# First attention of a linear-attention and two-MLP kernel: another order of its query steps and first transfers

## The chip, the cores and the metric

The kernel runs on one NeuronCore of one Trainium2 chip. The metric is the device time of one execution in microseconds (us); the times shown are medians of several runs. Engines are named as in the profile: PE (TensorE, matrix products), DVE (VectorE), ACT (ScalarE), POOL (GpSimd) and SP (SyncE, which here issues all transfers).

## The reference, cut to what matters

Linear attention with a feature map, and then two MLPs. Inputs are float32 for q, k, v and `w_phi`; the weights of the MLPs come as float64.

```python
# q, k, v: (4, 8, 576, 64); w_phi: (64, 128)
def phi(x):
    proj = einsum('bhsd,df->bhsf', x, w_phi)
    proj = proj - max(abs(proj), axis=-1, keepdims=True)
    return concatenate([exp(proj), exp(-proj)], axis=-1)
q_p, k_p = phi(q), phi(k)
kv  = einsum('bhsf,bhsd->bhfd', k_p, v);  z = sum(k_p, axis=2)
num = einsum('bhsf,bhfd->bhsd', q_p, kv)
den = einsum('bhsf,bhf->bhs', q_p, z)[..., None] + 1e-06
x = (num / den) as (2304, 512)
x = leaky_relu(x @ w_in, 0.01) @ w_out          # 512 -> 2048 -> 512
out = (silu(x @ w_gate) * (x @ w_val)) @ w3     # 512 -> 1536 -> 512
```

## The kernel before, in words

The work is cut by batch: four batches `b` of 576 tokens, each with eight heads in `NP = 4` pairs `j` (pair 0 to 3; two heads of 64 fill the 128 partitions). A batch's attention runs first over the keys (`k_steps`) and then over the queries (`q_steps`). The attention of batch 0 stands alone at the start of the program, at line 959 (`steps = k_steps(0) + q_steps(0)`); the attention of each later batch is spread over the MLP units of the batch before it, where PE always has other work.

**Keys of batch 0.** For each pair and each of five token tiles `s`: a projection of k with `w_phi` on PE (L161, into a bank of the PSUM pool `psm`, tag `pm`, 4 banks), the greatest absolute value (L166) and a subtraction (L59) on DVE, two exponentials on ACT (L177, L178), and two products with v that gather k'v and z in one bank of the pool `psa`, tag `pa`, 4 banks (L202). A pair ends with a copy (`kvz`, ACT), four transposes on PE (L240, `k_tr`) and a copy (`kvh`, ACT).

**Queries of batch 0.** For each pair: five projections on PE (`q_front`, L301, `pm` banks), each with a maximum on DVE (L304, into `mq`); then `q_m` turns the maxima into a row (`mrow`, L316 to L321, DVE, one buffer). Then, for two halves `t` of 288 tokens and the two heads `h`: `q_exp` multiplies the weights with the queries a second time, now with tokens along the free axis (L372, `pa` bank), takes the row off (L373) and makes two exponentials on ACT (L375, L376); `q_num` makes numerator and denominator (L393, `pa` bank), and ACT writes the denominator (L396). `q_fin` ends a half on DVE: transpose, reciprocal, transpose (L401, L403, L405), two products that free the two `pa` banks (L411), and the split of x in a high and a low part (`cp` on ACT into `xh`, `sub` on DVE into `xl`, L59). `xh` and `xl` of a pair are one fourth of the inner dimension of the first MLP layer.

**Weights.** Every weight block of 128 x 512 comes as float64 and is made float32 by ACT (L511, L512) and DVE (L513, L514, L519), then stored (`kept`, L524) and split (L541 on ACT, L59 on DVE). While the first attention runs, eight blocks of the gate weights (`early`, tag `gp`) and the first blocks of `w_in` (tag `wi`, loaded at L497) go this way. The MLP's products are made at L579, in `pm` banks, always in parts high x high, high x low, low x high.

**What sets the order.** The code gives an order of emission; the framework's scheduler, with priorities from that order and a timeline of its own, then fixes the order in which each engine has its instructions. An engine runs its instructions in that order. `early` stands under a lower priority than its place. In `q_steps` the order of emission is, for each pair: five projections, the maxima, the load of the next pair's queries, then the four exponential steps with the numerators one step behind. The queries and keys of a pair land in `raw`, a tag with two buffers; so the load of a pair can start when the pair two before it has made its last product from it. All loads and stores go through SP's queue in one order. At the start, SP issues k of pair 0 (L115), `w_phi` (L117) and three pieces of v (L123).

## Time and profile before

| | us |
|---|---|
| median of 3 timed runs | 1099.75 (1099.22 to 1103.96) |
| profiled execution | 1096.49 |
| its span, first to last instruction | 1094.7 |
| first matmul | 4.03 |
| PE busy, of the span | 1065.8 |
| DVE busy | 822.9 |
| ACT busy | 640.4 |
| granted TensorE clock | 1.0 in all 40 slices |

A share of the whole span is an average over stages of different kinds. The first attention fills about the first 88 us; the MLPs, with the other three attentions among them, fill the rest. In the first part PE, DVE and ACT all have work, and which of them is late changes from stage to stage; this is read from the busy times by stretch and from the waits in the timeline. A PE that is busy is not a PE at its peak, as matmuls are pipelined and their ends are modelled.

### The profile page before, as it was taken

How to read it: one execution, taken by the hardware profiler on the slowest of the kernel's cores; microseconds unless marked ns; L12 is line 12 of the kernel's file. 1: busy time of each engine (PE TensorE's matmuls, PEld its weight loads, DVE VectorE, ACT ScalarE, POOL GpSimd, SP SyncE). 2: the span in 40 equal slices, each digit the busy share in tenths (PEclk: the TensorE clock that was granted, in tenths of full speed). 3: DMA queues.
4: the chain of work that ended last, by engine and by line, in shares of the span. 5: the costliest groups of instructions: out<-in, count | busy, mean ns of one | idle time of the engine just before them, and what ended most of it. 6: DMA issues, size and time to landing. Idle time of an engine off the chain costs nothing.

```text
span 1094.7 us, 20495 instructions
## 1 busy us (share of the span) xinstructions
PE 1065.8 (97%) x7608; PEld 1027.0 (94%) x7608; DVE 822.9 (75%) x1801; ACT 640.4 (58%) x1455; POOL 6.8 (1%) x28
## 2 busy tenths in 40 slices
PE   8889999899999999999999999999999999999998
PEld 6668999889989999999999999999999999999998
DVE  7997787889999877678687877757778653558473
ACT  7768976757756786647545366434554345426441
POOL 1000000000000000000000000000000000000000
PEclk9999999999999999999999999999999999999999
DMA  9736766345654865567483888787652657548642
GB/s 331 240 94 188 217 194 219 127 144 169 194 183 146 333 249 190 186 265 271 150 313 118 304 309 285 274 280 257 230 174 78 225 202 282 201 148 288 238 140 78
DMA packets 96402, 233.02 MB, mean 213 GB/s; under 512 B 20144, under 2 KB 20400, under 8 KB 96304
## 3 DMA queue, kind: packets, MB, share of 16 engines
q1 hardware_dynamic: 96304, 231.72, 61.6%
q8 instruction: 60, 0.98, 0.4%
q14 instruction: 38, 0.31, 0.1%
HBM read 163.00 MB, written 68.68 MB: 212 GB/s over the span
## 4 chain that ended last, share of the span: by engine, by line
PE 79%; DVE 7%; DMA 7%; ACT 3%; issue 2%; SPq 1%; DVEq 0%; ACTq 0%
PE pm L579 57%; PE pa L707 9%; DMA wr<-kept 4%; PE pa L393 4%; PE pa L202 3%; DMA wi<-in_w_dram 2%; PE pa L161 2%; PE pm L707 1%; DVE wr L514 1%; DVE wr L519 1%; DMA wi<-in_wv_dram 1%; PE pm L301 1%; DMA vhl<-parts 1%; PE pa L346 1%; DVE wr L59 1%
## 5 line engine op out<-in xcount | busy, mean ns | idle before, releaser
L579 PE MATMUL pm<-xh,wi 128*128 128x288 f32 x1920 | 408.1, 298 | 3.0 <-DVE es L618 2.2
L579 PE MATMUL pm<-gp,wo 128*128 128x288 f32 x2352 | 349.0, 297 | 7.3 <-DVE acc L644 7.1
L579 PEld LDWEIGHTS pm<-gp,wo 128*128 128x128 f32 x2352 | 323.4, 188 | 11.7 <-DVE acc L644 8.4
L579 PEld LDWEIGHTS pm<-xh,wi 128*128 128x128 f32 x1920 | 313.8, 188 | 7.9 <-DVE es L618 2.8
L579 PE MATMUL pm<-xl,wi 128*128 128x288 f32 x960 | 284.1, 297 | 0.0
L579 PEld LDWEIGHTS pm<-xl,wi 128*128 128x128 f32 x960 | 180.4, 188 | 2.0 <-issue 0.8
L644 DVE TENSOR_TENSOR acc<-pm,acc 128x288 f32<-128x288 f32 x160 | 70.1, 451 | 43.8 <-PE pm L579 43.1
L59 DVE TENSOR_TENSOR gp<-es,gp 128x576 fp32r<-128x576 f32 x98 | 73.6, 751 | 13.5 <-ACT gp L62 12.6
L62 ACT ACTIVATE gp<-es 128x576 fp32r<-128x576 f32 x98 | 68.0, 696 | 26.8 <-DVE es L625 23.9
L541 ACT ACTIVATE wi<-wr 128x512 fp32r<-128x512 f32 x80 | 51.1, 645 | 23.0 <-DMA wr<-kept 8.8
L59 DVE TENSOR_TENSOR wi<-wr,wi 128x512 fp32r<-128x512 f32 x80 | 54.6, 684 | 11.2 <-ACT wi L541 10.6
L59 DVE TENSOR_TENSOR fl<-ff,fh 128x512 fp32r<-128x512 f32 (+1 forms) x72 | 50.7, 714 | 13.2 <-ACT fh L62 12.2
L512 ACT ACTIVATE wi<-wi 128x512 int32<-128x512 uint32 x60 | 42.3, 704 | 28.1 <-DMA wi<-in_w_dram 14.3
L396 ACT ACTIVATE dn<-pa 64x288 f32<-64x288 f32 x64 | 26.1, 407 | 46.2 <-PE pa L393 45.4
L511 ACT ACTIVATE wr<-wi 128x512 f32<-128x512 f32 x60 | 41.7, 699 | 15.7 <-DMA wi<-in_w_dram 7.3
L605 ACT ACTIVATE es<-pm 128x288 f32<-128x288 f32 x96 | 39.7, 424 | 13.2 <-PE pm L579 12.6
L62 ACT ACTIVATE fh<-ff 128x512 fp32r<-128x512 f32 (+1 forms) x72 | 46.9, 670 | 0.6
L519 DVE TENSOR_TENSOR wr<-wr,wi 128x512 uint16<-128x512 uint16 x60 | 44.8, 748 | 0.4
L202 PE MATMUL pa<-ff,pk 128*128 128x256 f32 (+1 forms) x160 | 42.8, 383 | 1.5 <-issue 1.1
L513 DVE TENSOR_SCALAR wr<-wr 128x512 int32<-128x512 int32 x68 | 28.4, 419 | 18.7 <-ACT wr L511 18.6
L62 ACT ACTIVATE acc<-pm 128x288 f32<-128x288 f32 x64 | 26.4, 441 | 26.4 <-PE pm L579 26.1
L59 DVE TENSOR_TENSOR wo<-wr,wo 128x512 fp32r<-128x512 f32 x56 | 37.4, 681 | 5.5 <-ACT wo L541 3.9
(171 smaller groups left out, 1954.8 us busy)
## 6 DMA issues: line engine op xcount, KB each, us to landing
wi<-parts SPq DMA_DIRECT2D x80, 512.0 KB, 4.7
wr<-kept SPq DMA_DIRECT2D x116, 256.0 KB, 4.8
wo<-parts SPq DMA_DIRECT2D x49, 512.0 KB, 5.5
wi<-in_w_dram SPq DMA_DIRECT2D x44, 512.0 KB, 4.3
parts<-wi SPq DMA_DIRECT2D x40, 512.0 KB, 5.8
kept<-wr SPq DMA_DIRECT2D x68, 256.0 KB, 4.0
parts<-wo SPq DMA_DIRECT2D x28, 512.0 KB, 6.2
sums<-wr SPq DMA_DIRECT2D x40, 256.0 KB, 3.6
```

The costliest lines, as they stand in the source:

```text
L59: dve.tensor_tensor(out=o, in0=a, in1=b, op=ALU.subtract)
L62: act.activation(o, a, AF.Copy)
L202: pe.matmul(ps[:, 256 * h : 256 * h + 256], v[:n, h].rearrange("p a d -> p (a d)"), part[b, j, s][:n, h].rearrange("p a f -> p (a f)"), st ...
L393: pe.matmul(ps, w, x, start=(i == 0), stop=(i == len(ops) - 1))
L511: act.activation(t, high.bitcast(F32), AF.Abs, scale=REBIAS)
L512: act.activation(low, low.bitcast(U32), AF.Copy, scale=2.0**-29)
L519: dve.tensor_tensor(out=t16, in0=t16, in1=e16, op=ALU.add)
L541: i = act.activation(t[:, 0], r, AF.Copy)
L579: m = pe.matmul(ps, w, x[:, c], start=(i == 0), stop=(i == n - 1))
L605: act.activation(o, i, AF.Prelu, alpha=0.01)
L644: dve.tensor_tensor(out=acc[o][:, t], in0=ps, in1=acc[o][:, t], op=ALU.add)
L707: m = pe.matmul(ps, a, b, start=start and n == 0, stop=stop and n == 5, skip_group_check=True)
```

## The change

`load_k` issues `w_phi` ahead of the first keys, and these in two parts of 256 and 320 columns. `q_m` writes the row of pairs 1 and 3 into a buffer of the tag `es` (5 buffers) and that of pairs 0 and 2 into the one `mrow` buffer. `q_steps` (for batch 0 alone, the others use `q_steps_t`) emits the projections and maxima of pair j + 1 between the exponential steps of pair j, and loads the queries of pair j + 2 in the last of these steps; the first three steps of the queries are emitted with the last three steps of the keys. The diff, cut to its core:

```diff
     def load_k(b, j):
         raw["k", b, j] = t = T([P, S], F32, "raw", 2)
-        nc.sync.dma_start(out=t, in_=kT[b, j])
-        if not (b or j):
+        if b or j:
+            nc.sync.dma_start(out=t, in_=kT[b, j])
+        else:
             nc.sync.dma_start(out=wbd.rearrange("p h f -> p (h f)"), in_=w_phi)
+            nc.sync.dma_start(out=t[:, 0 : OFF[2]], in_=kT[b, j, :, 0 : OFF[2]])
+            nc.sync.dma_start(out=t[:, OFF[2] :], in_=kT[b, j, :, OFF[2] :])
...
-        r = mrow[b, j] = T([P, 18, 32], F32R, "mrow", 1)
+        r = mrow[b, j] = T([P, 18, 32], F32R, *(("es", 5) if j % 2 else ("mrow", 1)))
...
+        seq = [fronts(0, 0, 1), load(1) + fronts(0, 2, 3), fronts(0, 4) + maxima(0)]
+        last = []
         for j in range(NP):
-            seq.append([lambda j=j: q_front(b, j, 0), lambda j=j: q_front(b, j, 1)])
-            seq.append([lambda j=j: q_front(b, j, 2), lambda j=j: q_front(b, j, 3)])
-            nxt = (lambda j=j: load_q(b, j + 1)) if j + 1 < NP else (lambda: load_k(b + 1, 0) if b + 1 < B else None)
-            seq.append([lambda j=j: q_front(b, j, 4), lambda j=j: q_m(b, j), nxt])
...
+            seq.append(last + exps(j, 0, 0) + fronts(j + 1, 0, 1))
+            seq.append(exps(j, 1, 0) + nums(j, 0, 0) + fronts(j + 1, 2, 3))
+            seq.append(exps(j, 0, 1) + nums(j, 1, 0) + fronts(j + 1, 4))
+            seq.append(exps(j, 1, 1) + nums(j, 0, 1) + maxima(j + 1) + load(j + 2))
+            last = nums(j, 1, 1)
+        return seq + [last]
...
-    steps = k_steps(0) + q_steps(0)
+
+    one, two = k_steps(0), q_steps(0)
+    steps = one[:-3] + [a + b for a, b in zip(one[-3:], two[:3])] + two[3:]
```

Of the instructions, one transfer is added, and none is taken away; what the scheduler makes of the new emission is seen in the engines' orders. Line numbers after the change are higher by 3 from `load_k` on and by 12 from `q_steps_t` on (L304 is the projection L301, L375 and L376 are L372 and L373, L396 is L393, L243 is L240, L378 and L379 are the exponentials, L399 is L396, L523 and L524 are L511 and L512, L414 is L411). A name with its number is a buffer; `raw_403` and `raw_404` hold the queries of pair 0, `raw_477` and `raw_456` those of pair 1.

PE at the seam from keys to queries, before:

```order
L202 MATMUL pa_400<-ff_438,pk_340 128x256 x2
L240 MATMUL pa_448<-cst_sb,kvz_446 128x128 x4
L372 MATMUL pa_479<-raw_403,wbd 128x288
L372 MATMUL pa_485<-raw_403,wbd 128x288
L301 MATMUL pm_555<-wbd,raw_477 128x256
L301 MATMUL pm_559<-wbd,raw_477 128x256
L301 MATMUL pm_562<-wbd,raw_477 128x256
L301 MATMUL pm_565<-wbd,raw_477 128x256
L373 MATMUL pa_479<-mrow_475,sel 128x288
L373 MATMUL pa_485<-mrow_475,sel 128x288
```

and after:

```order
L205 MATMUL pa_401<-ff_439,pk_341 128x256 x2
L304 MATMUL pm_486<-wbd,raw_456 128x256
L304 MATMUL pm_490<-wbd,raw_456 128x256
L304 MATMUL pm_504<-wbd,raw_456 128x256
L304 MATMUL pm_507<-wbd,raw_456 128x256
L243 MATMUL pa_464<-cst_sb,kvz_454 128x128 x4
L375 MATMUL pa_480<-raw_404,wbd 128x288
L376 MATMUL pa_480<-mrow_478,sel 128x288
L375 MATMUL pa_493<-raw_404,wbd 128x288
L376 MATMUL pa_493<-mrow_478,sel 128x288
```

Four projections of pair 1 moved from behind the first score products of pair 0 to ahead of the last key pair's transposes.

DVE at the end of pair 1's first half (`pm_785` to `pm_795` before, `pm_686` to `pm_717` after, are projections of pair 3; `wr_847` and `wr_882` are weights in conversion), before:

```order
L321 TENSOR_TENSOR mrow_695<-mt_693,cst_sb 128x576
L405 STREAM_TRANSPOSE rb_630<-rc_628 128x288
L514 SCALAR_TENSOR_TENSOR wr_847<-gp_845,wr_847 128x512
L411 TENSOR_TENSOR xf_632<-pa_601,rb_630 64x288
L411 TENSOR_TENSOR xf_632<-pa_622,rb_630 64x288
L304 TENSOR_REDUCE mq_787<-pm_785 128x2
```

and after:

```order
L324 TENSOR_TENSOR mrow_651<-mt_649,cst_sb 128x576
L406 RECIPROCAL rc_612<-t_175_610 128x9
L531 TENSOR_TENSOR wr_882<-wr_882,gp_880 128x512
L307 TENSOR_REDUCE mq_688<-pm_686 128x2
L408 STREAM_TRANSPOSE rb_614<-rc_612 128x288
L404 STREAM_TRANSPOSE t_196_669<-dn_645 128x288
L307 TENSOR_REDUCE mq_688<-pm_690 128x2
L525 TENSOR_SCALAR wr_937<-wr_937 128x512
L307 TENSOR_REDUCE mq_688<-pm_714 128x2
L307 TENSOR_REDUCE mq_688<-pm_717 128x2
L414 TENSOR_TENSOR xf_616<-pa_589,rb_614 64x288
L414 TENSOR_TENSOR xf_616<-pa_606,rb_614 64x288
```

The two products that finish the half moved behind four maxima of pair 3.

ACT at the end of pair 3 (`wi_297` before and `wi_298` after are a weight block as it was loaded), before:

```order
L396 ACTIVATE dn_843<-pa_861 64x288
L375 ACTIVATE ff_881<-pa_878 128x288
L376 ACTIVATE ff_881<-pa_878 128x288
L511 ACTIVATE wr_1061<-wi_297 128x512
L512 ACTIVATE wi_297<-wi_297 128x512
L396 ACTIVATE dn_887<-pa_884 64x288
```

and after:

```order
L523 ACTIVATE wr_1062<-wi_298 128x512
L399 ACTIVATE dn_834<-pa_842 64x288
L524 ACTIVATE wi_298<-wi_298 128x512
L378 ACTIVATE ff_872<-pa_869 128x288
L379 ACTIVATE ff_872<-pa_869 128x288
L399 ACTIVATE dn_878<-pa_875 64x288
```

The two conversion steps moved from behind the last two exponentials to ahead of them.

## Rows read from the trace of the kernel before

**Rows 1.** The page's totals: busy us (share of the span) and instructions.

```profile
PE 1065.8 (97%) x7608; PEld 1027.0 (94%) x7608; DVE 822.9 (75%) x1801; ACT 640.4 (58%) x1455; POOL 6.8 (1%) x28
```

**Rows 2.** Busy us by stretch: PE, PEld, DVE, ACT, POOL, PEclk, DMA share, GB/s.

```profile
20.00:30.00 10.00, 9.38 (x44) 7.60 (x44) 8.47 (x19) 9.90 (x25) 0.83 (x3) 1.00 1.08 388
...
52.00:64.00 12.00, 9.55 (x38) 6.64 (x39) 11.55 (x31) 6.99 (x18) 0.00 (x0) 1.00 0.29 92
...
76.00:88.00 12.00, 10.74 (x50) 8.19 (x50) 10.05 (x25) 8.20 (x21) 0.00 (x0) 1.00 0.32 98
...
314.00:392.00 78.00, 75.68 (x552) 73.48 (x551) 67.88 (x146) 57.23 (x135) 0.00 (x0) 1.00 0.68 244
```

**Rows 3.** Timeline, PE: start, us, instruction, xrecords (two per float32 matmul), [idle before <-releaser].

```profile
41.29 0.65 PE L240 MATMUL pa<-cst_sb,kvz 128*128 128x128 f32 x4 [0.69 <-ACT kvz L62]
...
52.48 1.97 PE L301 MATMUL pm<-wbd,raw 128*128 128x256 f32 x8 [0.86 <-DVE xf L411]
...
58.83 1.24 PE L393 MATMUL pa<-ff,kvh 128*128 128x288 f32 x4 [0.86 <-ACT ff L376]
...
64.02 1.96 PE L301 MATMUL pm<-wbd,raw 128*128 128x256 f32 x8 [0.45 <-DMA raw<-in_qT_dram]
...
76.52 0.72 PE L372 MATMUL pa<-raw,wbd 128*128 128x288 f32 x2 [0.58 <-DVE xf L411]
...
86.69 0.53 PE L579 MATMUL pm<-xh,wi 128*128 128x288 f32 x2 [0.50 <-ACT xh L62]
```

**Rows 4.** Timeline of the start: SP's issue, DVE, PE.

```profile
1.17 0.42 SPq L117 DMA_DIRECT2D wbd<-in_w_phi_dram  x1
...
3.92 0.29 DVE L84 CAST wbd_h<-wbd 128x256 fp32r<-128x256 f32 x1 [3.92 <-DMA wbd<-in_w_phi_dram]
...
4.03 5.44 PE L161 MATMUL pm<-wbd,raw 128*128 128x256 f32 x12 [4.03 <-DMA wbd<-in_w_phi_dram]
```

**Rows 5.** Timeline, ACT: the first weight conversion; the first query exponential.

```profile
10.56 0.67 ACT L511 ACTIVATE wr<-wi 128x512 f32<-128x512 f32 x1 [1.23 <-DMA wi<-in_w_dram]
...
44.82 0.41 ACT L375 ACTIVATE ff<-pa 128x288 f32<-128x288 f32 x1 [1.10 <-PE pa L373]
```

**Rows 6.** Timeline, DVE, among the query pairs.

```profile
43.17 0.43 DVE L513 TENSOR_SCALAR wr<-wr 128x512 int32<-128x512 int32 x1 [1.40 <-ACT wr L511]
...
63.55 0.92 DVE L411 TENSOR_TENSOR xf<-pa,rb 64x288 f32<-64x288 f32 x2
64.73 0.42 DVE L304 TENSOR_REDUCE mq<-pm 128x2 f32<-128x256 f32 x1 [0.25 <-PE pm L301]
...
75.93 0.93 DVE L411 TENSOR_TENSOR xf<-pa,rb 64x288 f32<-64x288 f32 x2
```

**Rows 7.** SP's issues (timeline); landing of query loads; weight loads: KB each, median us.

```profile
48.62 0.33 SPq L132 DMA_DIRECT2D raw<-in_qT_dram  x1
...
60.58 0.33 SPq L132 DMA_DIRECT2D raw<-in_qT_dram  x1
...
70.05 0.33 SPq L497 DMA_DIRECT2D wi<-in_w_dram  x1
...
80.42 0.33 SPq L497 DMA_DIRECT2D wi<-in_w_dram  x1
...
DMA to landing us min/median/max: 2.7/3.3/9.5
...
wi<-in_w_dram SPq DMA_DIRECT2D x5, 512.0 KB, 4.2
```

**Rows 8.** Timeline, ACT, end of pair 3: last head's exponential, weight conversion behind it.

```profile
82.69 0.41 ACT L375 ACTIVATE ff<-pa 128x288 f32<-128x288 f32 x1 [0.27 <-PE pa L373]
...
84.62 0.67 ACT L511 ACTIVATE wr<-wi 128x512 f32<-128x512 f32 x1 [1.23 <-DMA wi<-in_w_dram]
```

**Rows 9.** Timeline, PE, from 314 to 392 us: its waits.

```profile
348.91 0.40 PE L579 MATMUL pm<-xh,wi 128*128 128x288 f32 x1 [0.57 <-DVE es L618]
...
362.50 3.71 PE L579 MATMUL pm<-gp,wo 128*128 128x288 f32 x26 [1.75 <-DVE acc L644]
```

More of the change, by code (lines that the diff above doesn't have):

```diff
@@ L421, in q_steps, with fronts, maxima, load @@
             return q_steps_t(b)
-        seq = []
-        for j in range(NP):
-            seq.append([lambda j=j: q_front(b, j, 0), lambda j=j: q_front(b, j, 1)])
-            seq.append([lambda j=j: q_front(b, j, 2), lambda j=j: q_front(b, j, 3)])
-            nxt = (lambda j=j: load_q(b, j + 1)) if j + 1 < NP else (lambda: load_k(b + 1, 0) if b + 1 < B else None)
-            seq.append([lambda j=j: q_front(b, j, 4), lambda j=j: q_m(b, j), nxt])
-            prev = None
-            for t in range(2):
-                for h in range(2):
-                    todo = [lambda j=j, h=h, t=t: q_exp(b, j, h, t)]
-                    if prev:
-                        todo += prev
-                    prev = [lambda j=j, h=h, t=t: q_num(b, j, h, t)]
-                    if h == 1:
-                        prev.append(lambda j=j, t=t: q_fin(b, j, t))
-                    seq.append(todo)
-            seq.append(prev)
-        return seq
+        def fronts(j, *tiles):
+            return [lambda s=s: q_front(b, j, s) for s in tiles] if j < NP else []
+        def maxima(j):
+            return [lambda: q_m(b, j)] if j < NP else []
+        def load(j):
+            if j < NP:
+                return [lambda: load_q(b, j)]
+            return [lambda: load_k(b + 1, 0)] if j == NP and b + 1 < B else []
+        def exps(j, h, t):
+            return [lambda: q_exp(b, j, h, t)]
+        def nums(j, h, t):
+            return [lambda: q_num(b, j, h, t)] + ([lambda: q_fin(b, j, t)] if h else [])
+        seq = [fronts(0, 0, 1), load(1) + fronts(0, 2, 3), fronts(0, 4) + maxima(0)]
+        last = []
+        for j in range(NP):
+            seq.append(last + exps(j, 0, 0) + fronts(j + 1, 0, 1))
[4 more added lines that the diff above has]
+        return seq + [last]
     def q_steps_t(b):
```

## The prediction

> **What bounds the kernel now.** I read the page's totals first: TensorE (PE) is busy for 97% of the span [rows 1]. So time can go only where PE stands idle, and a cheaper instruction elsewhere is worth nothing unless PE waits for it. Next I read the busy time of every engine by stretch [rows 2]. In 20 to 30 us, where the first attention's keys are worked on, ScalarE (ACT) is busy 9.90 of 10 us and the transfers run at 388 GB/s: ACT and DMA set the pace there. In 52 to 64 us, among the exponentials of the queries, VectorE (DVE) is busy 11.55 of 12 us while PE has 9.55: DVE sets the pace, and beside the attention it carries the conversion of weights (L513, L514, L519). In 76 to 88 us nothing is full (PE 10.74, DVE 10.05, ACT 8.20 of 12): a chain of waits does it.
>
> Third, the timeline of PE alone [rows 3] shows where it stands: one wait of 0.69 us at the seam from keys to queries (the transpose L240 waits for ACT's copy), then waits of 0.45 to 0.86 us by each pair of heads. I number the four pairs 0 to 3 as `j` does. These six rows make 3.9 us; two more of the same kind, 0.69 and 0.68 us before the last numerators of pairs 0 and 1, bring the waits of PE between 41 and 87 us to 5.3 us; 4.03 us before the first matmul come on top. **That is all the change can win in the attention**, since each engine still does the same work: the program built from the change has the same instructions, except one more DMA, and at the last numerator of pair 3 the same number of matmuls stands ahead on PE.
>
> **The change part by part.**
>
> *First transfers.* `w_phi` goes first, then 256 columns of k, then the other 320. Before, 288 KB of k and 128 KB of `w_phi` land before the first matmul at 4.03 us, and `w_phi` is issued second, at 1.17 us [rows 4]. Afterwards the second transfer is again issued at about 1.17 us, but only 128 KB stand before it instead of 288 KB. 160 KB at 388 GB/s [rows 2] are 0.4 us, so the first matmul starts some 0.4 us earlier (between 0, if the issue and not the bytes decides, and 0.8). DVE's four set-up copies, which begin at 3.92 us when `w_phi` is there, move by as much. What is late next: ACT, which runs in the program's order, has the first weight conversion (L511) at 10.56 us and waits 1.23 us there for its 512 KB [rows 5]. That transfer stands behind the same bytes in the same queue as before; the extra issue (0.42 us on SP [rows 4]) is hidden, since this queue has a backlog by then. ACT gets there sooner and waits longer, and from there ACT has hardly a gap until the keys are done. Kept: 0, with 0.5 us as the other end.
>
> *The seam.* In the order of PE four projections of pair 1 (L301) now stand before the transposes L240 of the last keys, where they stood behind the first score products of pair 0. In the trace such a group of four takes 1.96 us (the row at 64.02 in [rows 3]), so it covers the wait of 0.69 us; the first exponential, at 44.82 us on ACT after a wait of 1.10 us [rows 5], can start about 0.9 us earlier: projections to 42.2, transposes to 42.6, score product (0.5) and maximum (0.35) to 43.5, ACT at 43.9. DVE gains the same: its wait of 1.40 us for ACT at 43.17 us [rows 6] now has two maxima of 0.4 us ahead of it, and ACT's conversion stands before the copy of the transposes. Bounds: 0, if ACT's two conversions now ahead push the copy back, and 1.4. I take −0.9, by the first exponential's row.
>
> *Pair 1.* PE waits 0.86 us at 58.83 us for an exponential [rows 3]; ACT ran a conversion (0.67 us, as in [rows 8]) between the first two exponentials. That conversion now stands ahead of both, in time in which ACT waits anyway. Bounds 0 and 0.67; I take −0.4. What ends such a gap is a bank, too: the four `pa` banks hold the sums of pair 0's second half until DVE has finished it. Perfetto Trace Analysis of the Trainium skill (section Optimization Strategy) has a rule for this: one gap that repeats on the engine that should be full can mean that there is no buffer for the next tile. By that rule this term would be 0 and not −0.4, as the change adds no bank, and the sum +1.3 instead of +0.9. The row at 52.48 names DVE, but pair 2's queries, issued at 48.62 us with some 3.3 us to land [rows 7], come only then too. Their load stays behind the last use of its buffer (there are two `raw` buffers), and on SP one more store (`kept`) is now issued ahead of it: so the projections of pairs 2 and 3 **do not** come between the exponentials of the pair before. PE's order of pairs 1 and 2 is otherwise the old one.
>
> *Pair 2.* On DVE the two products that finish the first half of pair 1 (L411, at 63.55 us, just before the first maximum of pair 3 at 64.73 [rows 6]) now stand behind four maxima of pair 3. These need pair 3's queries, whose load starts when pair 1's last score product is done (60.58 us) and takes about 3.3 us [rows 7]. With the 1.3 us won so far the load is there at 62.6, the four projections at 64.5, the last of the four maxima with what stands between at about 65.7, L411 at 65.7 to 66.6: two us later than before. These products free the PSUM banks for pair 2's scores. PE has nine matmuls of the first layer and the fifth projection in between (1.6 us), so it does not stand idle for all of it. What ends pair 2 is then the weights: the conversion queued on DVE ahead of pair 2's L411 (75.93 us [rows 6]) needs a 512 KB load that was issued at 70.05 us, after an earlier conversion has freed its buffer, and takes 4.2 us [rows 7]; by the new order that load starts at about 69.9 us. Load 74.0, ACT's two conversion steps and an exponential pair to 75.7, DVE's step to 76.1, L411 at 76.1. So the 1.3 us are given back here: +1.2, between 0 and +1.5.
>
> *Pair 3.* On ACT a conversion (L511) that waits for a load stood behind the last exponentials of pair 3: these ran at 82.69 us, and L511 waited 1.23 us for the load, to 84.62 [rows 8]. It now stands ahead of the last two exponentials, with a sum (L396) and the second conversion step between. The load starts when DVE has done the previous conversion (80.42 us [rows 7]); that one stands two places earlier on DVE, and by the durations between I put the load's start at 79.0 and its landing at 83.2. Then L511 and L512 at 0.67 us each and one sum (0.41) come before the exponentials: 84.9 instead of 82.69. Queued behind are the numerators of the last half, and the sum that DVE needs for the first half. PE takes the first layer up again at 86.69 us [rows 3] when the first half's x is copied; I put that at 87.7: +1.0. Bounds: 0, if the load lands before the exponentials' turn, and +2.7, if it lands at 84.6 as now.
>
> *Later.* From there to 170 us small permutations, and in 314 to 392 us a different interleaving around the second attention's end. PE is busy 75.68 of 78 us there [rows 2], and its two waits are 0.57 and 1.75 us [rows 9]. Bounds −2.3 and +2.3; I take 0, since both wait for DVE, which has the same work.
>
> **Sum:** 0 − 0.9 − 0.4 + 1.2 + 1.0 + 0 = +0.9 us. The profiled execution took 1096.49 us (span 1094.7 and 1.8 around it), so it would take 1097.4; the median of the three timed runs is 1099.75, and on that the forecast is **1100.6 us**.
>
> **Rivals.** *A, the projections fill the waits.* PE's 5.3 us of waits all close and 0.5 us of the start is kept: 5.8 us off, 1093.9 us. For it: PE is at 97%, DVE gets rid of a wait, and the second `mrow` buffer takes away a real wait of the maxima for the scores. Against it: DVE at 11.55 of 12 us in 52 to 64, and the two `raw` buffers. *B, the change does not do what it says.* The scheduler had hoisted the projections already; nothing moves beyond 0.5 us: 1099.7 us. For it: two of the waits in [rows 3], at 52.48 and 76.52 us, end with the DVE product that frees a bank, and projections use other banks. Against it: queries land just before 52.48 and 64.02, and at the seam the order on PE has changed. The rule of the Trainium skill named under pair 1 would lead here if all the gaps were of its kind; the trace bears it out for the one at 76.52. *C, ACT is blocked at the end.* The load before L511 starts no earlier than 80.42 us, and ACT stands until 84.6 with the last two exponentials behind it: these run at 86.3, 3.6 us late, and the last sums (L396) and x follow. Some 2.7 us reach PE, and with the first 1.2 us given back in pair 2 the time is 1102.5; if the late stretch [rows 9] doubles its waits as well, 1104.8. It decides from the point where the load starts later than 79 us.
>
> **How the numbers follow.** My forecast 0.45, A 0.25, B 0.12, C 0.18. About 0.5% is what a measurement of this kernel can tell from no change, that is 5.5 us: 1094.25 and 1105.25 are the marks. A lies on the lower one; I count 0.15 of it as faster, and 0.02 from the late stretch. Of C 0.07 pass the upper mark. Faster 0.17, same 0.76, slower 0.07. The range reaches from A's time less a little to C with the late stretch: 1093.0 to 1104.8.
>
> **What would show it.** Right: the first matmul at 3.5 to 3.7 us, and L511 still at 10.5; the first exponential (L375) near 43.9; no wait of PE before the transposes; waits of PE for pair 2's and 3's queries as before; L411 of pair 1's first half after 65 us; L511 ahead of the last exponentials, with a wait for its load. Wrong: a steady first layer well before 84 us (A), the last exponentials at their old time (pair 3's term), or a gain before 10 us that is still there at 40 us.

## The result, and the profile after

The changed kernel takes **1105.62 us** (median of 17 runs, 1100.79 to 1109.47); the kernel before took 1099.22 in as many runs beside it. The ratio is 1.0059, with a 95% interval from 1.0042 to 1.0076: slower by 0.6%, 6.4 us. The forecast was 1100.6 with a range to 1104.8, so the time lies outside; it is also past the prediction's upper mark of 1105.25, and to that the prediction gave 0.07. The profiled execution took 1105.04 us (span 1102.9) at a mean granted clock of 0.994. That clock is a term that the prediction did not have at all. One execution of the kernel before, among those timed beside the experiments, was in a slow state (1295.34 us at a mean clock of 0.754) and is in none of the numbers below.

The page's totals after, beside [rows 1]: PE is busy for 5 us more, with the same number of instructions.

```profile
PE 1071.0 (97%) x7608; PEld 1031.9 (94%) x7608; DVE 823.8 (75%) x1801; ACT 640.0 (58%) x1455; POOL 6.6 (1%) x28
```

Busy us by stretch after, columns as in [rows 2]; the stretches of [rows 2] and four short ones:

```profile
12.00:14.00 2.00, 0.70 (x2) 0.30 (x2) 1.97 (x5) 1.86 (x5) 0.00 (x0) 1.00 1.03 391
14.00:16.00 2.00, 1.77 (x4) 1.50 (x5) 2.00 (x7) 2.00 (x6) 0.00 (x0) 0.54 1.02 405
16.00:18.00 2.00, 2.00 (x7) 1.59 (x7) 1.64 (x4) 0.48 (x2) 0.32 (x1) 0.61 1.04 414
20.00:30.00 10.00, 9.81 (x45) 7.38 (x43) 6.79 (x16) 9.93 (x25) 1.03 (x4) 1.00 1.08 389
52.00:64.00 12.00, 9.78 (x40) 6.71 (x38) 11.18 (x31) 7.67 (x20) 0.00 (x0) 1.00 0.29 86
76.00:88.00 12.00, 9.86 (x48) 7.44 (x46) 8.56 (x20) 8.30 (x21) 0.00 (x0) 1.00 0.48 153
88.00:92.00 4.00, 3.27 (x9) 2.36 (x9) 3.42 (x10) 1.94 (x5) 0.00 (x0) 0.66 0.41 84
314.00:392.00 78.00, 75.27 (x542) 72.47 (x541) 70.58 (x154) 54.07 (x122) 0.00 (x0) 1.00 0.63 219
```

The first three rows and the last but one hold the surprise. PE is busy for 0.70 of the 2 us from 12 to 14; behind that the granted clock (PEclk) is 0.54 and 0.61, so for most of 14 to 18 us it is at 1.2 GHz and not at 2.4. PE reads as full from 16 to 18 us with 7 matmul records; in the same two microseconds the kernel before made 11. The same happens behind a wait at 88 us. The page's slices don't show it: each prints a 9, which stands for 90% or more, and a slice of 27.6 us with 3.4 us at the half clock is still at 0.94. The mean clock of the core (0.994 against 1.000) does.

The timeline of PE after, its waits in the first attention, beside [rows 3, 4]:

```profile
3.41 4.33 PE L164 MATMUL pm<-wbd,raw 128*128 128x256 f32 x10 [3.41 <-DMA raw<-in_kT_dram]
...
13.20 0.70 PE L164 MATMUL pm<-wbd,raw 128*128 128x256 f32 x2 [1.57 <-DVE ff L59]
14.23 2.08 PE L205 MATMUL pa<-ff,pk 96*128 96x256 f32 x4 [0.33 <-ACT ff L181]
...
32.21 0.70 PE L164 MATMUL pm<-wbd,raw 128*128 128x256 f32 x2 [2.23 <-DVE ff L59]
...
35.66 0.70 PE L164 MATMUL pm<-wbd,raw 128*128 128x256 f32 x2 [0.98 <-DVE ff L59]
...
60.36 1.24 PE L396 MATMUL pa<-ff,kvh 128*128 128x288 f32 x4 [0.86 <-ACT ff L379]
...
88.73 1.81 PE L396 MATMUL pa<-ff,kvh 128*128 128x288 f32 x4 [1.88 <-ACT ff L379]
...
94.83 0.67 PE L205 MATMUL pa<-ff,pk 128*128 128x256 f32 x2 [1.53 <-ACT ff L176]
```

The first matmul comes at 3.41 us, 0.6 earlier; by 13.2 us PE is at the 29th record, as before (before: 13.11, behind a wait of 0.18, and 13.26 behind 0.96 in a second execution of the same kernel). The time won at the start has become a wait in one piece.

ACT after, beside [rows 5, 8], DVE, beside [rows 6], and SP's weight loads, beside [rows 7]:

```profile
10.96 0.67 ACT L523 ACTIVATE wr<-wi 128x512 f32<-128x512 f32 x1 [2.83 <-DMA wi<-in_w_dram]
...
47.56 0.42 ACT L378 ACTIVATE ff<-pa 128x288 f32<-128x288 f32 x1
...
86.16 0.67 ACT L523 ACTIVATE wr<-wi 128x512 f32<-128x512 f32 x1 [1.33 <-DMA wi<-in_w_dram]
...
87.28 0.67 ACT L524 ACTIVATE wi<-wi 128x512 int32<-128x512 uint32 x1
87.97 0.41 ACT L378 ACTIVATE ff<-pa 128x288 f32<-128x288 f32 x1
...
93.42 0.67 ACT L524 ACTIVATE wi<-wi 128x512 int32<-128x512 uint32 x1 [1.96 <-DMA wi<-in_w_dram]
```

```profile
11.66 0.43 DVE L525 TENSOR_SCALAR wr<-wr 128x512 int32<-128x512 int32 x1 [2.00 <-ACT wr L523]
12.12 0.69 DVE L526 SCALAR_TENSOR_TENSOR wr<-wi,wr 128x512 int32<-128x512 int32 x1
12.73 0.42 DVE L59 TENSOR_TENSOR ff<-pm,mk 128x256 f32<-128x256 f32 x1
...
68.55 0.92 DVE L414 TENSOR_TENSOR xf<-pa,rb 64x288 f32<-64x288 f32 x2
...
78.94 0.93 DVE L414 TENSOR_TENSOR xf<-pa,rb 64x288 f32<-64x288 f32 x2
```

```profile
72.58 0.33 SPq L509 DMA_DIRECT2D wi<-in_w_dram  x1
...
82.05 0.33 SPq L509 DMA_DIRECT2D wi<-in_w_dram  x1
```

At the start ACT waits for the first weight block (10.96 us), DVE waits for ACT, and the subtraction that frees PE's bank is behind that (12.73). At the end of pair 3 ACT twice stands for a load: at 86.16 us ahead of the last exponentials (87.97 instead of 82.69) and at 93.42 ahead of the exponentials of the next batch's keys.

### The profile page after: what moved, and what is told of

Same layout as the page of the kernel before. It is cut to its first block, busy times and chain, and to the rows that moved or that the text cites. A ratio compares the mean times of both kernels' runs of the same rounds, so it can differ in the third digit from the quotient of the medians.

```text
span 1102.9 us, 20494 instructions
## 1 busy us (share of the span) xinstructions
PE 1071.0 (97%) x7608; PEld 1031.9 (94%) x7608; DVE 823.8 (75%) x1801; ACT 640.0 (58%) x1455; POOL 6.6 (1%) x28
## 4 chain that ended last, share of the span: by engine, by line
PE 75%; DMA 11%; DVE 8%; ACT 3%; issue 2%; SPq 1%; DVEq 0%; ACTq 0%
PE pm L591 53%; PE pa L719 9%; DMA wr<-kept 5%; PE pa L396 3%; PE pa L205 3%; DMA wi<-in_w_dram 3%; PE pm L719 1%; PE pa L164 1%; DVE wr L531 1%; DVE wr L59 1%; DVE wr L526 1%; DMA wi<-in_wv_dram 1%; ACT wr L523 1%; DMA vhl<-parts 1%; PE pa L349 1%
## 5 line engine op out<-in xcount | busy, mean ns | idle before, releaser
L524 ACT ACTIVATE wi<-wi 128x512 int32<-128x512 uint32 x60 | 41.4, 690 | 27.9 <-DMA wi<-in_w_dram 13.4
L399 ACT ACTIVATE dn<-pa 64x288 f32<-64x288 f32 x64 | 26.0, 407 | 50.6 <-PE pa L396 49.9
L523 ACT ACTIVATE wr<-wi 128x512 f32<-128x512 f32 x60 | 40.8, 683 | 20.8 <-DMA wi<-in_w_dram 10.9
L396 PE MATMUL pa<-ff,kvh 128*128 128x288 f32 x128 | 37.7, 418 | 4.8 <-ACT ff L379 4.7
```

What stands on the lines that cost most here:

```text
L396: pe.matmul(ps, w, x, start=(i == 0), stop=(i == len(ops) - 1))
L523: act.activation(t, high.bitcast(F32), AF.Abs, scale=REBIAS)
L524: act.activation(low, low.bitcast(U32), AF.Copy, scale=2.0**-29)
```

## The experiments

In all of them the lag is taken against a second profiled execution of the kernel before (the first experiment), at three places: the first query exponential (44.98 us there), the last pair of exponentials (82.22), and the start of PE's 901st matmul record (171.79), in the steady first layer: from the 832nd record on, PE's order is the same in all kernels up to some 310 us. The wait is PE's one between 11 and 15 us. The mean clock is that of all timed executions.

| kernel | first matmul | wait | lag first exp. | lag last exp. | lag 901st | mean clock | median us | ratio, 95% interval |
|---|---|---|---|---|---|---|---|---|
| before, again | 4.04 | 0.96 | 0 | 0 | 0 | 0.9976 | 1099.80 | 1.0001 (0.9988 to 1.0014) |
| changed | 3.41 | 1.57 | 2.58 | 5.75 | 7.21 | 0.9948 | 1105.62 | 1.0059 (1.0042 to 1.0076) |
| changed, again | 3.48 | 2.46 | 4.15 | 7.63 | 9.21 | 0.9950 | 1107.10 | 1.0060 (1.0040 to 1.0080) |
| transfers alone | 3.80 | 0.77 | 1.12 | 5.01 | 5.33 | 0.9940 | 1110.05 | 1.0091 (1.0071 to 1.0111) |
| query steps alone | 4.00 | 1.12 | 0.29 | 0.21 | 0.34 | 0.9976 | 1097.43 | 0.9986 (0.9969 to 1.0004) |
| w_phi first alone | 4.14 | 0.29 | -0.34 | -0.35 | -0.28 | 0.9969 | 1098.45 | 0.9995 (0.9979 to 1.0011) |
| before, transfers cut at 128 | 3.15 | 0.18 | -0.17 | -0.11 | 0.12 | 0.9976 | 1098.27 | 0.9982 (0.9968 to 0.9996) |
| before, transfers cut at 448 | 4.04 | 1.41 | 0.84 | 5.11 | 5.80 | 0.9955 | 1108.33 | 1.0080 (1.0060 to 1.0100) |
| changed, cut at 128 | 3.12 | 0.75 | -0.47 | -0.45 | -0.38 | 0.9977 | 1096.80 | 0.9983 (0.9965 to 1.0002) |
| changed, conversion put back | 3.42 | 2.19 | 6.15 | 7.42 | 6.92 | 0.9903 | 1110.58 | 1.0100 (1.0082 to 1.0117) |
| changed, one load's wait gone | 3.48 | 2.15 | 4.71 | 6.31 | 9.43 | 0.9950 | 1104.74 | 1.0042 (1.0023 to 1.0061) |
| changed, two loads' waits gone | 3.85 | 1.47 | 2.52 | 4.29 | 3.80 | 0.9957 | 1102.88 | 1.0027 (1.0011 to 1.0044) |
| changed, w_phi last | 4.54 | 0.61 | 1.15 | 4.23 | 5.53 | 0.9943 | 1105.65 | 1.0074 (1.0046 to 1.0101) |

**Control: the kernel before again.**

> The kernel before, unchanged, as a control for the spread of its times and of the granted TensorE clock over many executions. In the profiled execution of the kernel before the granted clock was 1.000 throughout; in 17 executions of the changed kernel it was 0.992 to 0.998. Theory S (the changed start costs: the order of the first keys leaves gaps on PE behind which the clock falls): here the clock is 0.999 to 1.000 in nearly all executions, time ratio 1.000. Theory N (the clock falls in either kernel as it happens, and the two profiled executions only differ by chance): here 0.992 to 0.998 too, in most executions.

Measured: 0.995 to 1.000, mean 0.9976. The truth lies between the theories. The first profile of before, at 1.000 throughout, was a rare one: 8 of 105 executions of this kernel are. But the changed kernel is lower (0.9949 in the mean of 23 executions, against 0.9970).

**Which part of the change.** The first transfers alone, the query steps alone, and `w_phi` first with k in one piece:

```diff
 # transfers alone, on the kernel before
-        nc.sync.dma_start(out=t, in_=kT[b, j])
-        if not (b or j):
+        if b or j:
+            nc.sync.dma_start(out=t, in_=kT[b, j])
+        else:
             nc.sync.dma_start(out=wbd.rearrange("p h f -> p (h f)"), in_=w_phi)
+            nc.sync.dma_start(out=t[:, 0 : OFF[2]], in_=kT[b, j, :, 0 : OFF[2]])
+            nc.sync.dma_start(out=t[:, OFF[2] :], in_=kT[b, j, :, OFF[2] :])
 # w_phi first alone, on the kernel before
-        nc.sync.dma_start(out=t, in_=kT[b, j])
         if not (b or j):
             nc.sync.dma_start(out=wbd.rearrange("p h f -> p (h f)"), in_=w_phi)
+        nc.sync.dma_start(out=t, in_=kT[b, j])
 # query steps alone, on the kernel before: the new q_steps and the new buffer in q_m
 # (not the last part of the change: the queries are emitted behind all the keys)
```

> The kernel before with the new order of the first transfers alone (w_phi first, k of pair 0 in two parts), query steps as before. Theory S: the first exponential of the queries runs at 47 to 48 us instead of 44.8, as in the changed kernel (47.56), the granted clock shows the lower level somewhere between 12 and 20 us, and most of the cost is here: 3 to 5 us slower. Theory Q (the new query order costs, as in rival C: ACT stands before the last exponentials of pair 3 for a weight load): no difference here, first exponential at 44.3 to 45, last exponential pair near 82.7 us, ratio 0.999 to 1.001.

> The kernel before with the new query steps alone (projections and maxima of pair j+1 among the exponentials of pair j, the second row buffer), first transfers as before. Theory S: the start is that of the kernel before, the first exponential comes at 43.9 to 44.8 us, and the whole is within 1.5 us of before. Theory Q: the last exponentials of pair 3 start at 85 us or later (before 82.69, changed kernel 87.97) behind the weight conversion, and the whole is 3 to 5 us slower.

> The kernel before with w_phi issued ahead of k of pair 0, k in one piece, query steps as before. It tells the two halves of the transfer change apart. Theory S: the order of the first keys on PE and DVE stays that of before (six projections first), so no cost: within 1 us of before, no gap on PE between 11 and 18 us that before hasn't. If the order of the transfers itself costs, and not the cut of k, it is as slow as the kernel with both. Theory Q: no difference.

The transfers alone cost 10 us, more than the whole change; the query steps alone nothing, nor `w_phi` first. So it is the cut of k, or what the scheduler makes of it. The run of the query steps leaves out the part of the change that emits the first three steps of the queries with the last three of the keys; that part is in a run below that has all parts and another cut. ACT at the end of pair 3 with the query steps alone:

```profile
82.43 0.41 ACT L375 ACTIVATE ff<-pa 128x288 f32<-128x288 f32 x1 [0.27 <-PE pa L373]
...
84.32 0.67 ACT L520 ACTIVATE wr<-wi 128x512 f32<-128x512 f32 x1 [1.18 <-DMA wi<-in_w_dram]
```

and with the transfers alone:

```profile
84.80 0.67 ACT L514 ACTIVATE wr<-wi 128x512 f32<-128x512 f32 x1 [1.97 <-DMA wi<-in_w_dram]
...
87.23 0.41 ACT L378 ACTIVATE ff<-pa 128x288 f32<-128x288 f32 x1
```

The moves at the seam and at pair 3 that the prediction reads off the orders of the changed program are there **without** the new query steps, and with these alone they are not: in the first attention the query steps change the row's buffer and leave the orders of PE and ACT alone (on DVE three pairs of neighbours change places). The scheduler had put the projections of the next pair there all along, and what moved them, and many rows of ACT and DVE, came with the cut of k. That the cause is an earlier readiness of the first keys in the scheduler's own timeline is likely, but no run shows that timeline.

Theory S was half wrong: the first exponential comes 1.1 us late here and not 2 to 3, there is no fall of the clock at 12 to 20 us, and yet the kernel is slow. Theory Q's place was right and its cause (the query steps) wrong.

Together with the cut, the query steps do change something, far behind: between the 1801st and the 2401st record (304 to 398 us) the kernel with the transfers alone loses 4.0 us against the first profile of before and the changed kernel wins 1.4. These 5.4 us, from one execution of each, are more than the 4.4 us between their medians. The one with the transfers alone has a wait there that the changed one hasn't, and at 374 us a fall of the clock:

```profile
373.14 3.18 PE L582 MATMUL pm<-gp,wo 128*128 128x288 f32 x16 [2.78 <-DVE acc L647]
```

**The head or the rest.** Two other cuts separate the two, since the scheduler makes other orders of them: at 128 columns the head of the keys is that of the slow kernel and the rest that of before; at 448 it is the other way round.

```diff
-            nc.sync.dma_start(out=t[:, 0 : OFF[2]], in_=kT[b, j, :, 0 : OFF[2]])
-            nc.sync.dma_start(out=t[:, OFF[2] :], in_=kT[b, j, :, OFF[2] :])
+            nc.sync.dma_start(out=t[:, 0 : OFF[1]], in_=kT[b, j, :, 0 : OFF[1]])   # 448: OFF[4]
+            nc.sync.dma_start(out=t[:, OFF[1] :], in_=kT[b, j, :, OFF[1] :])
```

> The kernel before with the new transfers, but k of pair 0 cut after 128 columns instead of 256; query steps as before. By the programs' orders this one shares the head of the slow transfer kernel (five projections, then products, up to PE's 37th matmul) and has everything from there to the end of the first attention, the seam and pair 3 included, in the order of before. Theory H (the head of the keys costs): first exponential at 46 us or later, 150 us into the run 3 to 5 us behind before. Theory O (the order further on costs: the keys' end, the seam, and ACT standing behind a weight load at pair 3): first exponential at 44.5 to 45.2, last exponentials of pair 3 near 82.5, within 1 us of before at 150 us; the whole within 2 us, the rest being the later stretch at 310 to 390 us, which is permuted here too.

> The kernel before with the new transfers, but k of pair 0 cut after 448 columns; query steps as before. By the programs' orders it has six projections first, as before, and from PE's 36th matmul on every engine has the order of the slow transfer kernel. Theory H: no cost, first exponential at 44.5 to 45.2, whole within 2 us of before. Theory O: as slow as the slow transfer kernel: first exponential near 46, last exponentials of pair 3 at 87, 4 to 5 us behind before at 150 us and 7 us (at an equal granted clock) in all.

As theory O says, with a margin: cut at 128 the lag is 0.12 us at the 901st record, cut at 448 it is 5.80. PE of the kernel cut at 128 starts at 3.15 us, earliest but one of all, and loses nothing behind:

```profile
3.15 5.01 PE L164 MATMUL pm<-wbd,raw 128*128 128x256 f32 x10 [3.15 <-DMA raw<-in_kT_dram]
...
12.57 1.13 PE L205 MATMUL pa<-ff,pk 96*128 96x256 f32 x4 [0.18 <-ACT ff L181]
```

Then the changed kernel with all its parts and that one number changed:

> The changed kernel with one number changed: k of pair 0 is cut after 128 columns instead of 256. All its parts (w_phi first, k in two transfers, the new query steps, the second row buffer) are there. By the programs' orders it has the rows of before from PE's 38th matmul to the end of the first attention. If the order of the engines is what costs, and not the parts of the change: 1097 to 1100, a ratio of 0.996 to 1.000, granted clock 0.997 or above. If the query steps or the extra transfer cost by themselves: 1103 or more.

1096.80 us, 0.9983 of before: 8.4 us less than the changed kernel by the ratios. With all parts of the change there, the order of the first attention is that of the kernel before cut at 128, but for the row's buffer; so none of the parts costs by itself, and the cost lies in the orders that the cut at 256 or 448 brings. Against before, the interval reaches to 1.0002, so it is no more than level with it; the kernel before with the transfers cut at 128 is at 0.9982, with 0.9996 as its upper end. These are the best two of the study.

**ACT behind the loads.** First the conversion ahead of the last exponentials was put back behind them:

```diff
+        if (b, j, h, t) == (0, NP - 1, 1, 1):
+            for i in (i0, i1):                      # the last two exponentials
+                tc.stamp_issue_order_token(i.ins, "tail")
...
+        if key == tail:                             # the ninth weight block
+            for i in (i0, i1):
+                tc.stamp_issue_order_token(i.ins, "tail")
...
+    slots[-1] = late                                # its emission, after the query steps
+    splits(-1)
```

> The changed kernel with the weight conversion that stands ahead of pair 3's last two exponentials on ACT put behind them, by an order token; the last conversion is emitted after the query steps. The first 52 matmuls and the first transfers are as in the changed kernel; between there and the exponentials' end some rows permute. If the block on ACT is the larger part of the loss: the last exponentials start at 83.5 to 85.5 us (changed 87.97, before 82.69), and at 150 us the kernel is 2 to 3.5 us ahead of the changed one, about 1102 in all. If the loss is in the keys alone and what is late at pair 3 is only handed on: last exponentials at 86 us or later and no more than 1 us gained at 150 us.

A miss: 1110.58 us. Moving an emission changed the scheduler's order of the keys as well, and the first exponential is 6.15 us late. The order at the end is as intended, and there the lag grows by 0.77 us from the first exponential to the 901st record (changed kernel 4.63). But as a test of one thing it is spoilt. A cleaner one leaves the emission alone and takes away what the conversion waits for, so that one block, or two, of the first layer has another block's weights:

```diff
         r = w64.pop(key)
+        if key == order[8]:          # two blocks: in order[8:10]
+            r = seen[0]              # the raw tile of the eighth block
+        seen[:] = [r]                # two blocks: in the else branch
```

> The changed kernel with the cause of ACT's wait at pair 3 taken away: the ninth weight block's conversion reads the raw tile of the eighth, which has landed long before, instead of its own (so one block of the first layer has the wrong weights; the same instructions run). The order of every engine is that of the changed kernel up to the end of pair 2's exponentials; behind it the tail permutes, since the conversion no longer waits. If ACT's block is a cost of its own: the last exponentials of pair 3 run 3.5 to 4.5 us behind those of before instead of 5.7 (84 to 86.5 us, by what the keys hand on), the lag at 150 us falls by 2 to 3 us, and the time is about 1103 to 1104. If the lag of the keys is all there is, 150 us and the total stay as in the changed kernel, 1105 to 1107.

> The changed kernel with both waits of ACT for weight loads around pair 3's end taken away: the ninth and the tenth weight block's conversions read the raw tile of the eighth, which has landed (two blocks of the first layer have the wrong weights; the same instructions run). Orders are those of the changed kernel up to the end of pair 2's exponentials. With only the ninth's wait gone, the tenth's took its place (2.85 us before ACT's eviction of the first layer, PE idle for 2.77 us at 95.6) and the lag behind before at 150 us was no smaller. If ACT's standing for these loads is the loss of the query phase: from the first exponential to 150 us the lag grows by 1.5 us or less (changed kernel 4.6, one block 4.7), and the time is 1101 to 1103 at the changed kernel's clock. If the third wait in the row takes it over again: the growth stays at 4 us or more.

With one wait gone, the lag across pair 3 grows no more (from 6.56 us at pair 2's last exponentials, 79.39 against 72.83, to 6.31), but the 901st record is no earlier. The wait for the tenth block has taken over, ahead of the first layer's evictions (L620), in ACT and PE:

```profile
94.45 0.65 ACT L527 ACTIVATE wi<-wi 128x512 int32<-128x512 uint32 x1 [2.85 <-DMA wi<-in_w_dram]
```

```profile
95.59 0.61 PE L594 MATMUL pm<-xh,wi 128*128 128x288 f32 x1 [2.77 <-ACT es L620]
```

So that expectation failed (the time, 1104.74 us, is also above the 1103 to 1104 expected). With both waits gone, PE's last wait before the steady first layer is 0.24 us:

```profile
91.09 0.40 PE L595 MATMUL pm<-xh,wi 128*128 128x288 f32 x1 [0.24 <-ACT es L621]
```

From the first exponential to the 901st record the lag grows by 1.28 us instead of 4.63, which is 3.35 us less. Not all of it stays. Right behind, PE has two waits for gate weights that ACT and DVE split, which the changed kernel hasn't:

```profile
181.02 0.40 PE L595 MATMUL pm<-gp,wo 128*128 128x288 f32 x1 [0.56 <-ACT gp L62]
181.82 2.40 PE L595 MATMUL pm<-gp,wo 128*128 128x288 f32 x16 [0.39 <-DVE gp L59]
```

From the first exponential to the 961st record the lag grows by 2.78 us here and by 4.83 in the changed kernel; in the last run below, which has the changed kernel's order there and no fall of the clock between the keys and 217 us, by 4.38. So **ACT standing for two weight loads costs 1.6 to 2.1 us that last** in the profiled executions. Orders behind pair 2's exponentials permute too in this run, so the two waits are not the only difference. The median is 2.7 us below the changed kernel's, and the ratio to before falls from 1.0059 to 1.0027 (3.5 us by the ratios, whose intervals just overlap), a part of it with the mean clock (0.9957 against 0.9948).

**The clock.** The changed kernel again, and with `w_phi` behind the keys:

```diff
-            nc.sync.dma_start(out=wbd.rearrange("p h f -> p (h f)"), in_=w_phi)
             nc.sync.dma_start(out=t[:, 0 : OFF[2]], in_=kT[b, j, :, 0 : OFF[2]])
             nc.sync.dma_start(out=t[:, OFF[2] :], in_=kT[b, j, :, OFF[2] :])
+            nc.sync.dma_start(out=wbd.rearrange("p h f -> p (h f)"), in_=w_phi)
```

> The changed kernel again, beside the others on the same chip, for its level and for the places where the granted clock falls. If the dips at 14.2 and 89.3 us of its profiled execution come from its own gaps on PE (11.6 to 13.2, 86.9 to 88.7 us), they need not come in each execution, but the mean granted clock stays at 0.994 to 0.996, below the 0.997 of before; if they were chance, it is at 0.997. The time is 1104 to 1106 us.

> The changed kernel with w_phi issued behind the two parts of k instead of ahead of them: the same bytes stand ahead of the first weight block, and from PE's 36th matmul on every engine has the changed kernel's order; only the first matmul comes later, at 4.0 us instead of 3.4. If the earlier start is what opens the gap on PE before 13.2 us (PE has done its work sooner and then waits for the first weight block all the same): the gap shrinks from 1.57 to about 1 us, the granted clock stays at its upper level between 12 and 20 us, the first exponential comes at 46 to 46.5 us instead of 47.56, and the time is 1.5 us less than the changed kernel's, about 1104. If the gap comes from the order of the engines and not from the start: the gap and the time stay, 1105 to 1107.

The changed kernel again takes 1107.10 us, above the 1104 to 1106 expected, at the mean clock expected. Its second profile has a longer wait, as the first weight block landed 0.7 us later, and then a longer stretch at the half clock:

```profile
13.88 1.22 PE L164 MATMUL pm<-wbd,raw 128*128 128x256 f32 x2 [2.46 <-DVE ff L59]
```

```profile
14.00:16.00 2.00, 2.00 (x5) 1.55 (x6) 2.00 (x6) 2.00 (x7) 0.00 (x0) 0.50 1.04 422
...
18.00:20.00 2.00, 2.00 (x6) 1.56 (x5) 0.84 (x3) 0.60 (x2) 0.31 (x1) 0.50 1.01 356
```

In the same two microseconds the kernel with the transfers alone, whose engines have the same order up to PE's 107th matmul, made nearly twice as many matmuls at the full clock, behind a wait of 0.77 us:

```profile
14.00:16.00 2.00, 1.90 (x9) 1.50 (x9) 2.00 (x7) 2.00 (x6) 0.32 (x1) 1.00 1.03 413
```

At PE's 61st record the three are 1.59 (changed), 3.23 (again) and 0.16 us (transfers alone) behind before. So one such stretch costs 1.4 us there. ACT carries it on: its copy behind the first pair's products waits 1.85 us in the changed kernel,

```profile
18.33 0.60 ACT L62 ACTIVATE kvz<-pa 128x512 f32<-128x512 f32 x1 [1.85 <-PE pa L205]
```

and 0.21 with the transfers alone,

```profile
16.77 0.60 ACT L62 ACTIVATE kvz<-pa 128x512 f32<-128x512 f32 x1 [0.21 <-PE pa L205]
```

and from there to the first exponential ACT is 1.43 to 1.49 us behind. On PE the difference is gone for a while, since with the transfers alone PE waits 1.77 us for a piece of v at 26.01 us; at the first exponential it is 1.46 us again.

Of the 13 executions in the table and the first of before, the clock fell between 13 and 16 us in the five with the longest waits (1.47 to 2.46 us) and stayed up in the others (at most 1.41). But the length of a wait does not settle it: behind the wait of 2.23 us at 32.21 in the first profile of the changed kernel the clock stayed up, behind one of 2.23 at 33.83 in its second it fell; with the transfers alone it stayed up behind the 1.77 us at 26.01. No rule is drawn from this.

With `w_phi` last, the profile came out as expected: a wait of 0.61 us (1 expected), clock at 1.00 between 12 and 20 us, first exponential at 46.13, span 1100.9. The timed runs did not follow: 1105.65 us, where 1104 was expected, and a mean clock of 0.9943. That the earlier start opens the gap fits this profile, but is not shown by it: the kernel cut at 448 starts at 4.04 us and waits 1.41, and two executions of the kernel before wait 0.18 and 0.96. And the start is not what keeps the clock low over many executions. A line through all 219 timed executions of these kernels, each about its kernel's mean, gives 0.83 us for 0.001 of mean clock. By that some 1.8 us of the 6.0 between the means (1105.6 and 1099.6) go with the clock, and 4.2 us are left at an equal clock.

## Why the prediction was wrong, point by point

The terms, profiled execution against profiled execution of before, each from one place of the timeline to the next:

| term | forecast | measured | from |
|---|---|---|---|
| start and keys, to the last product | 0 | +3.7 | its last record starts at 40.23, then 43.92 |
| seam, to the first exponential | -0.9 | -1.0 | 44.82, 47.56 |
| pairs 0 and 1 | -0.4 | -0.8 | last exponentials 61.57, 63.52 |
| pair 2 | +1.2 | +2.0 | 73.31, 77.29 |
| pair 3 and the first layer | +1.0 | +2.6 | 82.69, 87.97; 901st record 172.44, 179.00 |
| 304 to 398 us | 0 (2.3 either way) | -1.4 | 1801st to 2401st record: 87.17, 85.72 |

Together +5.1 instead of +0.9. The profiled spans differ by 8.2; the other 3.1 us come where the clock falls at 219 and 984 us (the lag grows by 1.7 and 1.4 us there), and before's profiled execution had no such falls; its second one has them (at 213 and 977 us).

*Start and keys: this step failed.* What it says of the start is right: the first matmul at 3.41 us, L511 (now L523) at 10.96 and not earlier, nothing kept at 13.2 us. It then took the keys to be the same from there: "from there ACT has hardly a gap until the keys are done". That holds before (0.75 us in two gaps, from 11 us to the last keys' exponentials) and not after (3.6 us in three: 1.85, 0.83 and 0.96). The order of the keys had changed on every engine that works on them, and PE waits 3.6 us in four pieces between 20 and 36 us (the two longest stand above), where before had five short ones of 1.4 us together. In the kernels with this order and no fall of the clock there, that last record starts at 42.48 us (transfers alone), 42.49 (`w_phi` last) and 42.19 (cut at 448): 2.0 to 2.3 us for the order. The other 1.4 us are the clock. The prediction showed three places of the orders and priced those; the largest loss lay at a place that it did not show.

*The clock: a term that was missing.* The forecast read 1.0 in the profile of before and held it for a constant. The Trainium skill (TensorE: Matmul & The Clock Gate, Part 1) says that the default state is throttled and that activity releases it; of the default at the start no row here tells (the windows print 1.00 from 0 us on), but behind the waits above the trace shows the lower level, 1.2 GHz, and then the upper one again. The same page (Terms) prices time at the lower level with the missing share of the clock; for the stretch that begins in the second window above and is 3.4 us long in the record that is 1.7 us, an estimate; the runs show 1.4 to 1.5.

*Seam: right,* in mechanism and size: PE has no wait before the transposes, and the first exponential follows the last key product 1.0 us sooner.

*Pairs 0 and 1: sign right, size low.* The wait that the step meant to shorten is still there, 0.86 us at 60.36; the gain lies in pair 0, where the wait before its last numerators is gone. The rule of the Trainium skill that would have made this term 0 is not borne out by the sum; the gap at 60.36 stayed, as it would have it, but the row names ACT's exponential and not a bank as what ended it.

*Pair 2: mechanism right, mis-sized.* L411 (L414) of pair 1 ran at 68.55, after 65 as forecast. The load that was to start at 69.9 started at 72.58, and pair 2's L414 ran at 78.94 and not at 76.1; the cost was 2.0 and not 1.2.

*Pair 3: this is rival C.* The load before L511 started at 82.05 us, later than 79, and ACT stood for it (the rows at 82.05 and 86.16 above). The price of C, 2.7 us, comes near the 2.6 of the table; the experiments show 3.35 us for the two loads together up to the 901st record, of which 1.6 to 2.1 last. That a second load stands behind the first was not seen. C had a chance of 0.18, and its condition (79 us) hung on a chain that only worked out if nothing before it came late. Its time, 1102.5, was too low as well, since it too put the start and the keys at 0.

*Rival A* did not come: PE's waits among the query pairs did not close. They make 5.5 us between 44 and 89 us, as they did between 41 and 87 before (5.3 in the prediction, which left out one of 0.20).

*Rival B is true of half the change.* In the first attention the query steps do what B says: nothing, since the scheduler had hoisted the projections already. The prediction took the difference of the two programs' orders for the effect of the edit that speaks of these rows. It was the effect of another edit, three lines long and 40 us earlier.

## What to carry to other kernels

Where a scheduler with a timeline of its own sets the order, no line of a diff owns the rows that move: build each part alone and compare the orders before a term is given to a part, and then price the orders everywhere they differ, not at the places of which the diff speaks. A cut or a transfer that lets work start 0.6 us earlier can reorder the next 100 us; trying two other cuts costs little and here was worth some 8 us. Work that starts earlier while its next input does not come earlier turns into a wait of PE in one piece, behind which the clock can fall. And what is won at one place is to be read again further on: of 3.35 us won by taking two waits away, waits at 181 us took more than a third back.

## What the runs showed of the hardware that was not expected

The granted clock falls in the middle of a kernel whose PE is 97% busy. Behind waits of PE of 1.5 to 3.6 us it often goes to 0.50, for 3.4 or 6.8 us of the record, but behind others of that length it stays up; once, in the kernel cut at 448 at 78.87 us, it falls with no wait above 1.19 us near it. Executions of one program differ in it. The kernel before has a wait at 212 us in both profiles, of 2.89 us with no fall in the first,

```profile
212.51 1.72 PE L579 MATMUL pm<-gp,wo 128*128 128x288 f32 x11 [2.89 <-DVE acc L644]
```

and of 3.24 us with a fall behind it in the second:

```profile
211.63 2.75 PE L579 MATMUL pm<-gp,wo 128*128 128x288 f32 x14 [3.24 <-DVE acc L644]
```

These two profiles have one order, so they give the price. The second is 0.88 us ahead at the end of this wait and 0.65 us behind at the 1201st record; at the end of the wait at 977 us it is 1.52 us behind, and then 3.03. A fall of 3.4 us costs 1.5 us at either place, near the 1.4 at the start of the changed kernel. The mean clock of the kernel before tells how many of them an execution had: its second profile, with two, is at 0.997, the one of the query steps alone, with one, at 0.998. Of the 105 executions 8 are at 1.000, 30 at 0.998, 39 at 0.997 and 28 lower, and their times differ by it: 0.83 us for 0.001 of the mean clock. It stays open why the orders that lose time in the first attention have a lower mean clock (0.990 to 0.996) even where the profiled execution shows no fall at the start, as with the transfers alone and with `w_phi` last.
